# The second phase of a retention and two-layer gated kernel in a new order: early weight casts a chain ahead, x loads and block 5's eviction moved

## The chip, the cores and the metric

One core of a Trainium2 chip runs the whole program. The metric is the device time of one execution in microseconds (us). PE is the matrix engine TensorE, DVE is VectorE, ACT is ScalarE, POOL is GpSimd, and SP is SyncE, which here issues every DMA. PEld is the loading of weights into PE.

## What is computed

The program is three computations in a row, on 3072 tokens of 512 features:

```python
attn_out = _attn_ref(q, k, v)                      # decayed linear attention, 4 batches, 8 heads
x = transpose(attn_out).reshape(3072, 512)
h = x @ w_in;  x = (h * sigmoid(1.702 * h)) @ w_out          # 2048 wide
y = (sigmoid(x @ w_gate) * (x @ w_val)) @ w_out2             # 1536 wide
```

The change touches the last line, and the seam between the last two. All matrices are float32.

## The kernel before, in words

**Two phases.** The first (`units`, lines 702 to 754) works off attention and the first gated layer, six blocks of 512 tokens, and stores its result x to the DRAM tiles `x2d0` to `x2d5`. The second (lines 758 to 805) computes the last layer from them in three groups `g` of 1024 tokens, two blocks each. Every float32 product is made of three matmuls: each operand is split into a rounded high part and a low part (a cast on ACT, then a subtraction on DVE or POOL), and high times high, low times high and high times low are summed in a PSUM bank. In names, a final h or l tells the parts: `oh` and `ol` are the layer's weights, `xoh` and `xol` its input, `g2h` and `g2l` the gated values, `woh` and `wol` the output weights.

**Rounds and chains.** A group has three rounds `r`, and a round four chains: gate and value (`m` 0 and 1) for each of two pairs `p`. They are numbered through from 0 to 35; this text calls the four of a round its first to fourth chain. A chain multiplies a 2 by 2 block matrix by another with seven block products instead of eight (a Winograd scheme), each of six matmuls of 512 columns. In the order of PE: A11 B11 (`begin`), A12 B21, S2 T2, S1 T1, S3 T3 (`middle`), A22 T4, S4 B22 (`finish`). S1 to S4 are sums of weight blocks, made by `sums` on POOL; T1 to T4 are sums of x blocks. Intermediate results are taken off the bank `pa` between products: `m1` after A11 B11, `u2` after S2 T2 and `u3` after S3 T3, each a copy on ACT. The product that follows on the same bank adds to it and must wait for the copy.

**Weights of a chain.** `load_chain` brings them (`raw8`), `sums` adds the S blocks, and `split_chain` casts them in two pieces: the early one (S1, S2, A11, A12; 1024 columns; `oh0`, with the low part `ol0` by DVE) and the late one (S3, A22, S4; 768 columns; `oh1`, with `ol1` by POOL). The early piece of chain n + 1 is cast at the head of chain n's `middle`:

```python
        ahead = n + 1 < len(chains)
        if ahead and n > 0:
            rest = split_chain(n + 1, False)
```

and `rest()`, DVE's subtraction, follows before S1 T1. The results of four blocks of a chain go through `consume`: a sigmoid for a gate chain, and for a value chain a multiply by it, a cast to `g2h` and a subtraction to `g2l`. `split_out2` makes `woh` (ACT) and `wol` (POOL) from the loaded `wor`, at the end of each chain.

**The end of a round.** The last chain's `finish` stands among the output products (`out_products`): eight blocks of 128 tokens (`tt`), each over the round's four pieces of 128 features, in three rotating banks `po`. `evict` copies or adds each to `part`; in a group's last round it adds into `ost2` and stores to the output. There, `prep_x` of the next group is drawn in between: it loads x blocks (`xt`), forms T1 to T4 on POOL and splits them, in steps that `next(xs)` takes, two after each eviction.

**Order.** Every engine works off its instructions in the order in which the program lists them (`manual_schedule`), and so does SP with the DMAs. A tile that takes the place of an earlier one waits for all accesses of that one.

## Time and profile before

| | us |
|---|---|
| median of 3 runs | 1241.9 |
| lowest and highest run | 1239.98, 1242.96 |
| the profiled execution | 1237.37 |
| its span | 1235.6 |
| PE busy in the span | 1191.6 |
| DVE, ACT, POOL busy | 815.1, 537.8, 537.4 |

The span runs from the first to the last instruction; 1.8 us of the execution lie around it. Matmul records overlap: one lasts about 0.39 us, and the next begins about 0.23 us after it began, so PE counts as busy without a pause. A row of the timeline gives the start, the duration, the engine, the line, the operation with what it writes and reads, and in brackets the idle time of the engine before it and what ended that. In the list of waits a row names who waited for whom, the sum, how often, and the longest.

### The profile page before, as it was taken

To read this page: it belongs to the slowest core of one execution; us is meant where nothing else is said; L and a number is where in the kernel's file an instruction comes from. 1 tells how busy PE (TensorE), PEld (TensorE's weight loads), DVE (VectorE), ACT (ScalarE), POOL (GpSimd) and SP (SyncE) were. 2 spreads that over 40 slices of the span, in tenths; PEclk is the share of its full clock that TensorE was granted. 3 is DMA by queue.
4 is the path that set the end of the run, shared out by engine and by line. 5 is a ranking of instruction groups with operands and counts; after the bars stand their busy time and mean duration, and the time that the engine had idled before them with its cause. 6 is when DMAs were issued, how large, how long until landed. Compare 5 with 4: busy or idle time off the path is not lost.

```text
span 1235.6 us, 15997 instructions
## 1 busy us (share of the span) xinstructions
PE 1191.6 (96%) x5916; PEld 947.7 (77%) x5916; DVE 815.1 (66%) x1049; ACT 537.8 (44%) x948; POOL 537.4 (43%) x398
## 2 busy tenths in 40 slices
PE   6899999999999999999998999998999999999998
PEld 5666768877788787787886787876787877787877
DVE  5999998788687777765782626366636366535454
ACT  5334444344444444444553535253626163626151
POOL 4666773323232332322464616165616156625230
PEclk9899999999999999999999999999999999999999
DMA  8554244533334424303002202033202033212111
GB/s 301 202 175 151 84 154 161 198 117 134 118 119 137 137 94 157 125 18 103 26 1 86 85 25 75 25 107 128 77 26 78 25 97 117 91 37 63 41 35 68
DMA packets 62430, 123.47 MB, mean 100 GB/s; under 512 B 6800, under 2 KB 16016, under 8 KB 62352
## 3 DMA queue, kind: packets, MB, share of 16 engines
q1 hardware_dynamic: 62352, 122.46, 29.9%
q8 instruction: 46, 0.75, 0.2%
q14 instruction: 32, 0.26, 0.1%
HBM read 98.31 MB, written 24.12 MB: 99 GB/s over the span
## 4 chain that ended last, share of the span: by engine, by line
PE 73%; DVE 10%; issue 6%; POOL 4%; ACT 3%; DMA 3%; SPq 1%; POOLq 0%; DVEq 0%; ACTq 0%
PE pa L512 15%; PE acc L379 5%; PE pd L512 5%; PE h L275 5%; PE h L273 5%; PE h L274 5%; PE acc L380 5%; PE acc L381 5%; PE po L630 4%; PE po L629 4%; PE po L628 4%; PE pb L512 3%; DVE cva L236 2%; PE acc L375 2%; DVE g2l L542 1%
## 5 line engine op out<-in xcount | busy, mean ns | idle before, releaser
L266 POOL TENSOR_TENSOR wl<-wraw,wh 128x512 fp32r<-128x512 f32 x112 | 161.4, 1442 | 327.7 <-ACT wh L265 321.8
L273 PE MATMUL h<-xh,wh 128*128 128x512 f32 x384 | 155.4, 405 | 2.7 <-DVE xl L190 1.3
L275 PE MATMUL h<-xh,wl 128*128 128x512 f32 x384 | 152.6, 397 | 0.1
L274 PE MATMUL h<-xl,wh 128*128 128x512 f32 x384 | 151.8, 395 | 0.2 <-DVE xl L190 0.2
L380 PE MATMUL acc<-gh,wl 128*128 128x512 f32 x352 | 138.8, 394 | 4.8 <-POOL wl L266 4.8
L379 PE MATMUL acc<-gh,wh 128*128 128x512 f32 x352 | 142.4, 405 | 0.8 <-ACT sg L283 0.8
L381 PE MATMUL acc<-gl,wh 128*128 128x512 f32 x352 | 137.3, 390 | 0.0
L283 ACT ACTIVATE sg<-h 128x512 f32<-128x512 f32 x88 | 52.6, 598 | 188.7 <-PE h L275 188.5
L504 POOL TENSOR_TENSOR ol<-raw,oh 128x768 fp32r<-128x768 f32 x36 | 67.3, 1871 | 153.5 <-ACT oh L501 153.5
L512 PE MATMUL pa<-xoh,oh 128*128 128x512 f32 x288 | 115.0, 399 | 15.4 <-ACT u L571 11.0
L512 PE MATMUL pa<-xoh,ol 128*128 128x512 f32 x288 | 113.3, 393 | 0.8 <-DVE ol L504 0.8
L512 PE MATMUL pa<-xol,oh 128*128 128x512 f32 x288 | 113.8, 395 | 0.0
L628 PE MATMUL po<-woh,g2h 128*128 128x512 f32 x288 | 112.5, 391 | 1.2 <-DVE ost L521 1.2
L630 PE MATMUL po<-woh,g2l 128*128 128x512 f32 x288 | 112.5, 390 | 0.0
L629 PE MATMUL po<-wol,g2h 128*128 128x512 f32 x288 | 112.4, 390 | 0.0
L265 ACT CAST wh<-wraw 128x512 fp32r<-128x512 f32 x184 | 111.5, 614 | 0.2
L289 ACT CAST gh<-sg 128x512 fp32r<-128x512 f32 x88 | 54.6, 621 | 101.8 <-DVE sg L284 101.8
L284 DVE TENSOR_TENSOR sg<-h,sg 128x512 f32<-128x512 f32 x88 | 60.5, 687 | 54.4 <-ACT sg L283 54.4
L273 PEld LDWEIGHTS h<-xh,wh 128*128 128x128 f32 x384 | 72.8, 189 | 21.1 <-DVE xl L190 1.5
L275 PEld LDWEIGHTS h<-xh,wl 128*128 128x128 f32 x384 | 72.7, 189 | 19.0 <-POOL wl L266 1.5
L274 PEld LDWEIGHTS h<-xl,wh 128*128 128x128 f32 x384 | 72.7, 189 | 18.1 <-issue 1.9
L296 DVE TENSOR_TENSOR gl<-sg,gh 128x512 fp32r<-128x512 f32 x88 | 71.8, 816 | 17.2 <-ACT gh L289 17.2
(115 smaller groups left out, 2523.0 us busy)
## 6 DMA issues: line engine op xcount, KB each, us to landing
w<-in_w_dram SPq DMA_DIRECT2D x68, 512.0 KB, 3.6
in_t<-in_qkv_dram SPq DMA_DIRECT2D x96, 256.0 KB, 3.6
raw<-w2d SPq DMA_DIRECT2D x72, 256.0 KB, 3.1
w2d<-cva SPq DMA_DIRECT2D x36, 256.0 KB, 2.2
wor<-w2d SPq DMA_DIRECT2D x36, 256.0 KB, 2.6
xt<-x2d SPq DMA_DIRECT2D x24, 256.0 KB, 4.1
out_dram<-ost SPq DMA_DIRECT2D x24, 256.0 KB, 2.0
x2d<-ost SPq DMA_DIRECT2D x18, 256.0 KB, 2.9
```

Of the source, the lines that this page charges most:

```text
L265: nc.scalar.copy(wh, raw)
L266: lo_engine.tensor_tensor(out=wl, in0=raw, in1=wh, op=ALU.subtract)
L273: nc.tensor.matmul(bank[:, :n], wh[:, k, :], xh[:, k, :n], start=(k == 0), stop=False)
L274: nc.tensor.matmul(bank[:, :n], wh[:, k, :], xl[:, k, :n], start=False, stop=False)
L275: nc.tensor.matmul(bank[:, :n], wl[:, k, :], xh[:, k, :n], start=False, stop=(k == KC - 1))
L379: nc.tensor.matmul(a, wh[:, wc], gh[:, :n], start=st, stop=False)
L380: nc.tensor.matmul(a, wl[:, wc], gh[:, :n], start=False, stop=False)
L381: nc.tensor.matmul(a, wh[:, wc], gl[:, :n], start=False, stop=sp)
L512: nc.tensor.matmul(bank, w[:, kk], x[:, k, :], start=start and k == 0 and w is wh and x is xh, stop=stop and k == 1 and w is wl, skip_grou ...
L628: nc.tensor.matmul(bank, gh, wh, start=f == 0, stop=False)
L629: nc.tensor.matmul(bank, gh, wl, start=False, stop=False)
L630: nc.tensor.matmul(bank, gl, wh, start=False, stop=f == FR - 1)
```

## The change

It does five things in the second phase. The early cast of chain n + 2 is issued in `finish` of chain n, before the last cast or sigmoid of that chain (for the chain after a round's last, after the eviction of block 4), and only DVE's subtraction stays in `middle`. `split_out2` of a chain moves into the next chain's `middle`, behind the copy `u2`. In a round's last chain the low parts `g2l` are made in another order, the piece of the first token half first. The loads of `prep_x` are issued at the start of the third chain of a group's last round instead of the fourth, seven of them at once, three into a new pool `xu`, and its first two steps run before the last `finish`. The eviction of block 5 goes to `xt` tiles and stands behind `load_chain(1)` and `load_out(0)`. The first chain's special order (`begin` of the second chain after its `finish`) goes, and `sg`, `u2` and `c22` lose a buffer each.

```diff
@@ -380,10 +380,16 @@
             nc.tensor.matmul(a, wl[:, wc], gh[:, :n], start=False, stop=False)
             nc.tensor.matmul(a, wh[:, wc], gl[:, :n], start=False, stop=sp)
         w_t.pop((i, "out"), None)
-        if not sp:
-            return
+        if sp and i + 1 < len(units):
+            evict1(b, f)
+
+    def evict1(b, f):
+        acc = acc_t[b]
         for c in range(4):
-            t = half_t[b][c] if b in half_t else half_tile(c) if b < 2 else half_tile(3)
+            if b == len(blocks1) - 1:
+                t = p2["xt"].tile([P, 512], F32, name="xt", tag="xt")
+            else:
+                t = half_t[b][c] if b in half_t else half_tile(c if b < 2 else 3)
             if b in half_t:
                 nc.vector.tensor_tensor(out=t, in0=acc[c], in1=half_t[b][c], op=ALU.add)
             elif c % 2:
@@ -418,6 +424,7 @@
 
     def open_late():
         p2["w"].append(pool(ctx, "wo", 1, "left"))
+        p2["xu"] = pool(ctx, "xu", 3, "left")
         for name, bufs in (("g2", FR), ("wout", FR), ("part", TOK), ("tmp", 2)):
             p2[name] = pool(ctx, name, bufs, "left")
 
@@ -434,12 +441,24 @@
             [p2["x"].tile([P, 2, 512], F32R, name=f"{n}{j}", tag=f"{n}{j}") for n in ("xoh", "xol")] for j in range(7)
         ]
         xo[g] = hl
+        raws = [{}, {}]
+
+        def load(k, *js):
+            for j in js:
+                half, kk = {B11: (0, k), B12: (1, k), B22: (1, k + 2), B21: (0, k + 2)}[j]
+                name = "xu" if g and k and j != B21 else "xt"
+                raws[k][j] = p2[name].tile([P, 512], F32, name=name, tag=name)
+                nc.sync.dma_start(out=raws[k][j], in_=x2d[2 * g + half][:, kk, :])
+
+        load(0, B11, B12, B22, B21)
+        if g:
+            load(1, B11, B12, B22)
+        yield
         for k in range(2):
-            raw = {}
-            for j, half, kk in ((B11, 0, k), (B12, 1, k), (B22, 1, k + 2), (B21, 0, k + 2)):
-                raw[j] = p2["xt"].tile([P, 512], F32, name="xt", tag="xt")
-                nc.sync.dma_start(out=raw[j], in_=x2d[2 * g + half][:, kk, :])
-            yield
+            raw = raws[k]
+            if k:
+                load(1, *((B21,) if g else (B11, B12, B22, B21)))
+                yield
             for j in (T1, T2):
                 raw[j] = p2["xt"].tile([P, 512], F32, name="xt", tag="xt")
 
@@ -525,7 +544,7 @@
         g, r, p, m = chains[n]
         if m == 0:
             yield
-            sgt[p, which] = sg = tmp("sg", 5)
+            sgt[p, which] = sg = tmp("sg", 4)
             nc.scalar.activation(out=sg, in_=c, func=AF.Sigmoid)
             yield
             yield
@@ -542,7 +561,7 @@
         nc.vector.tensor_tensor(out=gl, in0=c, in1=gh, op=ALU.subtract)
         yield
 
-    carried = []
+    carried, whole, early = [], [], {}
 
     def begin(n):
         if n >= len(chains):
@@ -558,8 +577,8 @@
         a, m1 = cb[n]
         b, d = bank2("pb"), bank2("pd")
         ahead = n + 1 < len(chains)
-        if ahead and n > 0:
-            rest = split_chain(n + 1, False)
+        if ahead and (n + 1) not in early:
+            early[n + 1] = split_chain(n + 1, False)
         product(n, b, A12, B21, True, True)
         add(b, b, m1)
         while carried:
@@ -567,19 +586,20 @@
         c11 = consume(n, 0, b)
         next(c11)
         product(n, a, S2, T2, False, True)
-        u2 = tmp("u2", 2)
+        u2 = tmp("u2", 1)
         nc.scalar.copy(u2, a)
+        if whole:
+            whole.pop()
+            split_out2()
         next(c11)
-        if ahead and n > 0:
-            rest()
+        if ahead:
+            early.pop(n + 1)()
         product(n, d, S1, T1, True, True)
         product(n, a, S3, T3, False, True)
-        u3, c22 = tmp("u3", 1), tmp("c22", 2)
+        u3, c22 = tmp("u3", 1), tmp("c22", 1)
         nc.scalar.copy(u3, a)
         next(c11)
         add(c22, d, u3)
-        if n == 0:
-            split_chain(1, False)()
         cb[n] = [a, d, u2, c22]
 
     def finish(n, last):
@@ -589,12 +609,17 @@
         product(n, a, A22, T4, False, True)
         next(x22)
         next(x21)
-        next(x22)
+        if not last:
+            next(x22)
         product(n, d, S4, B22, False, True)
         next(x21)
+        if last:
+            next(x21)
         add(d, d, u2)
         next(x12)
-        next(x21)
+        next(x22 if last else x21)
+        if not last and n + 2 < len(chains):
+            early[n + 2] = split_chain(n + 2, False)
         next(x12)
         if last:
             next(x12)
@@ -757,6 +782,7 @@
 
         load_chain(1)
         load_out(0)
+        evict1(*units[-1])
         sums(1)
         xs = iter(())
         for n, (g, r, p, m) in enumerate(chains):
@@ -765,21 +791,21 @@
             load_chain(n + 2)
             if more:
                 load_out(n + 1)
-            if last and r == NR - 1 and g + 1 < NG:
+            if not last and r == NR - 1 and p == PAIRS - 1 and g + 1 < NG:
                 xs = prep_x(g + 1)
                 next(xs)
             middle(n)
             if n + 2 < len(chains) and not (last and r == NR - 1):
                 sums(n + 2)
+            if last:
+                for _ in range(2):
+                    next(xs, None)
             if not last:
-                if n > 0:
-                    begin(n + 1)
+                begin(n + 1)
                 rest = split_chain(n + 1, True)
                 finish(n, False)
                 rest()
-                split_out2()
-                if n == 0:
-                    begin(n + 1)
+                whole.append(n)
                 continue
             rest = split_chain(n + 1, True) if more else lambda: None
             split_out2()
@@ -798,10 +824,12 @@
                 evict(g, r, tt, ob[tt])
                 next(xs, None)
                 next(xs, None)
+                if tt == 5 and n + 2 < len(chains) and r == NR - 1:
+                    sums(n + 2)
+                if tt == 4 and n + 2 < len(chains) and r < NR - 1:
+                    early[n + 2] = split_chain(n + 2, False)
             for _ in xs:
                 pass
-            if n + 2 < len(chains) and r == NR - 1:
-                sums(n + 2)
             begin(n + 1)
```

**Place 1: ACT, from chain 5 (second of its round) into chain 6 (third).** `g2h` are the casts of chain 5's results, `oh0` is an early cast, `u2` chain 6's copy. Before:

```order
L540 CAST g2h_6650<-c22_6676 128x512
L540 CAST g2h_6650<-pa_6595 128x512
L540 CAST g2h_6648<-pd_6637 128x512
L617 CAST woh_6717<-wor_6551 128x512
L501 CAST oh0_6728<-raw8_6631 128x1024
L571 COPY u2_6745<-pa_6683 128x512
L529 ACTIVATE sg_6747<-pb_6726 128x512
```

and with the change:

```order
L559 CAST g2h_6649<-c22_6679 128x512
L559 CAST g2h_6649<-pa_6598 128x512
L520 CAST oh0_6718<-raw8_6633 128x1024
L559 CAST g2h_6647<-pd_6639 128x512
L590 COPY u2_6744<-pa_6686 128x512
L642 CAST woh_6746<-wor_6557 128x512
L548 ACTIVATE sg_6750<-pb_6728 128x512
L600 COPY u3_6765<-pa_6686 128x512
```

The cast of 1024 columns and `woh` no longer stand between the last `g2h` and `u2`; the cast stands one `g2h` earlier, and is one for chain 7, as the one before was, and `woh` follows `u2`.

**Place 2: SP, at the seam of the phases.** `x2d5` are the stores of block 5, `raw8` the weights of a chain, `wor` output weights. Before:

```order
L393 DMA x2d5_127<-ost_6041 128x512
L393 DMA x2d5_127<-ost_6044 128x512
L393 DMA x2d5_127<-ost_6047 128x512
L393 DMA x2d5_127<-ost_6050 128x512
L483 DMA raw8_6072<-w2d_130 128x2x256
L483 DMA raw8_6072<-w2d_130 128x512
L611 DMA wor_6075<-w2d_130 128x512
L483 DMA raw8_6080<-w2d_130 128x2x256
L483 DMA raw8_6080<-w2d_130 128x512
```

and with the change:

```order
L502 DMA raw8_6063<-w2d_130 128x2x256
L502 DMA raw8_6063<-w2d_130 128x512
L636 DMA wor_6066<-w2d_130 128x512
L399 DMA x2d5_127<-xt_6068 128x512
L399 DMA x2d5_127<-xt_6071 128x512
L399 DMA x2d5_127<-xt_6074 128x512
L399 DMA x2d5_127<-xt_6077 128x512
L502 DMA raw8_6083<-w2d_130 128x2x256
L502 DMA raw8_6083<-w2d_130 128x512
```

The loads for chain 1 and the first `wor` stand ahead of the four stores, and those of chain 2 behind.

**Place 3: DVE, in the last chain of the first group and after it.** `c22`, `pa` and `pd` are the chain's results, `xol0` to `xol6` low parts of the next group's x, `ost2` evictions. Before:

```order
L521 TENSOR_TENSOR c22_7332<-pd_7293,u3_7331 128x512
L538 TENSOR_TENSOR c22_7332<-c22_7332,sg_7247 128x512
L538 TENSOR_TENSOR pa_7229<-pa_7229,sg_7255 128x512
L542 TENSOR_TENSOR g2l_7307<-c22_7332,g2h_7306 128x512
L521 TENSOR_TENSOR pd_7293<-pd_7293,u2_7315 128x512
L538 TENSOR_TENSOR pd_7293<-pd_7293,sg_7258 128x512
L542 TENSOR_TENSOR g2l_7307<-pa_7229,g2h_7306 128x512
L542 TENSOR_TENSOR g2l_7305<-pd_7293,g2h_7304 128x512
L521 TENSOR_TENSOR ost2_7393<-po_7343,part_6446 128x512
L452 TENSOR_TENSOR xol0_7271<-xt_7284,xoh0_7270 128x512
L452 TENSOR_TENSOR xol1_7273<-xt_7290,xoh1_7272 128x512
```

and with the change:

```order
L540 TENSOR_TENSOR c22_7341<-pd_7301,u3_7340 128x512
L471 TENSOR_TENSOR xol0_7189<-xt_7202,xoh0_7188 128x512
L471 TENSOR_TENSOR xol1_7191<-xt_7208,xoh1_7190 128x512
L557 TENSOR_TENSOR c22_7341<-c22_7341,sg_7278 128x512
L557 TENSOR_TENSOR pa_7260<-pa_7260,sg_7286 128x512
L561 TENSOR_TENSOR g2l_7312<-pa_7260,g2h_7311 128x512
L540 TENSOR_TENSOR pd_7301<-pd_7301,u2_7320 128x512
L557 TENSOR_TENSOR pd_7301<-pd_7301,sg_7292 128x512
L561 TENSOR_TENSOR g2l_7312<-c22_7341,g2h_7311 128x512
L561 TENSOR_TENSOR g2l_7310<-pd_7301,g2h_7309 128x512
L540 TENSOR_TENSOR ost2_7410<-po_7360,part_6449 128x512
```

Two x subtractions come ahead of the chain's multiplies, and the low part of `pa` comes ahead of that of `c22`.

## Rows read from the trace of the kernel before

**Rows 1.** Busy time by engine (PE, PEld, DVE, ACT, POOL), second phase.

```profile
659.50:1235.60 576.10, 554.99 (x2389) 446.25 (x2387) 296.26 (x373) 241.94 (x400) 248.28 (x196) 1.00 0.21 69
```

**Rows 2.** List of waits, PE, from 655 us to the end.

```profile
PE pa L512 <- ACT u L571: 11.0, 11, 1.7
PE pa L512 <- ACT m L553: 2.3, 2, 1.2
PE pa L512 <- ACT oh L501: 1.4, 1, 1.4
PE po L628 <- DVE ost L521: 1.2, 2, 0.8
...
PE pa L512 <- DVE ol L504: 0.8, 1, 0.8
```

**Rows 3.** Timeline of PE, third chain of the second round.

```profile
751.98 0.39 PE L512 MATMUL pd<-xoh,ol 128*128 128x512 f32 x1
753.29 0.50 PE L512 MATMUL pa<-xoh,oh 128*128 128x512 f32 x1 [0.92 <-ACT u L571]
753.62 0.40 PE L512 MATMUL pa<-xol,oh 128*128 128x512 f32 x1
```

**Rows 4.** Timeline of ACT, same place.

```profile
750.70 0.59 ACT L540 CAST g2h<-pd 128x512 fp32r<-128x512 f32 x1 [2.49 <-DVE pd L538]
751.18 0.62 ACT L617 CAST woh<-wor 128x512 fp32r<-128x512 f32 x1
751.70 1.05 ACT L501 CAST oh<-raw 128x1024 fp32r<-128x1024 f32 x1
```

**Rows 5.** Timeline of DVE, same place.

```profile
747.49 1.83 DVE L542 TENSOR_TENSOR g2l<-c,g2h 128x512 fp32r<-128x512 f32 x1
...
749.96 0.70 DVE L538 TENSOR_TENSOR pd<-pd,sg 128x512 f32<-128x512 f32 x1
...
751.77 0.68 DVE L542 TENSOR_TENSOR g2l<-pd,g2h 128x512 fp32r<-128x512 f32 x1
752.78 1.47 DVE L504 TENSOR_TENSOR ol<-raw,oh 128x1024 fp32r<-128x1024 f32 x1 [0.33 <-ACT oh L501]
```

**Rows 6.** Timeline of POOL, same place.

```profile
746.92 1.85 POOL L504 TENSOR_TENSOR ol<-raw,oh 128x768 fp32r<-128x768 f32 x1 [1.20 <-ACT oh L501]
751.88 1.28 POOL L618 TENSOR_TENSOR wol<-wor,woh 128x512 fp32r<-128x512 f32 x1 [3.11 <-DMA raw<-w2d]
753.12 1.72 POOL L489 TENSOR_TENSOR raw<-raw 128x256 f32<-128x256 f32 x1
```

**Rows 7.** Timeline of POOL and DVE at two places of the first phase.

```profile
65.79 1.59 POOL L256 TENSOR_TENSOR wraw<-cva,cvb 128x512 f32<-128x512 f32 x1
65.82 0.41 DVE L233 TENSOR_SCALAR cva<-cva 128x512 uint32<-128x512 uint32 x1
...
162.13 1.30 POOL L266 TENSOR_TENSOR wl<-wraw,wh 128x512 fp32r<-128x512 f32 x1
162.15 1.55 DVE L233 TENSOR_SCALAR cva<-cva 128x512 uint32<-128x512 uint32 x1
```

**Rows 8.** First change of group: timeline of SP and DVE; DMA issues of the page.

```profile
843.56 1.81 SPq L441 DMA_DIRECT2D xt<-x2d  x4
848.73 0.68 DVE L521 TENSOR_TENSOR ost<-po,part 128x512 f32<-128x512 f32 x1
xt<-x2d SPq DMA_DIRECT2D x24, 256.0 KB, 4.1
```

**Rows 9.** Seam of the phases: timeline of POOL, SP and PE; DMA issues of the page.

```profile
655.56 2.52 POOL L266 TENSOR_TENSOR wl<-wraw,wh 128x512 fp32r<-128x512 f32 x2 [3.92 <-ACT wh L265]
666.83 1.18 SPq L483 DMA_DIRECT2D raw<-w2d  x2
669.99 0.50 PE L512 MATMUL pa<-xoh,oh 128*128 128x512 f32 x1 [0.68 <-ACT u L578]
raw<-w2d SPq DMA_DIRECT2D x72, 256.0 KB, 3.1
```

## The prediction

> **What bounds the kernel now.** I read the second phase alone, since the change leaves the first one's work as it is. The busy times of that stretch come first [rows 1]: PE works for 555.0 of 576.1 us, DVE, ACT and POOL for half of it or less. So PE sets the time, and only its pauses, some 21 us, can be won. The list of waits names them [rows 2]: 17 waits with 16.7 us of idle time, and one more of 0.7 that comes up under (c), 18 with 17.4; 14 of them are for copies that ACT takes off the bank `pa` (`u` of L571 and L578, `m`). The timeline of one of them shows what a wait costs [rows 3]: from 751.98 to 753.29 are 1.31 us and on to 753.62 another 0.33, where two matmuls would have begun 0.23 apart; that is 1.18 for 0.92 of idle time, or the idle time and 0.26. With that, all 18 cost 17.4 + 18 x 0.26 = 22.1 us, the most that this change can give.
>
> They lie at three places. (a) The third chain of each of the nine rounds waits for `u2`: the 11.0 us of [rows 2] less two waits of 1.7, so 7.6 + 9 x 0.26 = 9.9. (b) The two changes of group have those two, two for `m` (2.3) and two for `ost` (1.2): 6.9 + 6 x 0.26 = 8.5. (c) The seam of the phases has the other three, 2.9 + 3 x 0.26 = 3.7.
>
> **(a) The casts around `u2`.** ACT begins `g2h` at 750.70, then works off `woh` and the cast of 1024 columns [rows 4], and only then `u2`, which keeps PE until 753.29 [rows 3]. The new order of place 1 has neither ahead of `u2`: it starts where `woh` did, at 751.18, and takes what `g2h` takes, 0.59, until 751.77. PE could use it from 752.21 (751.98 + 0.23), so this wait goes, with 0.44 to spare. The moved cast falls into the 2.49 us in which ACT idled ahead of 750.70 [rows 4], and takes 1.05 of them. In a gate chain the cast must follow POOL's sums, and POOL now has `wol` in front of these: `wol` from at most 753.6, then two sums of at most 1.28 each, is 757.4. ACT gets to the cast at about 757.1 (18 matmuls after 752.21, a sigmoid of 0.6) and must have begun it by 759.2, so that it and the last sigmoid end before the next `u2` (36 matmuls after 752.21, 760.5). That costs nothing now, and 1 us for each us of POOL beyond 1.8. A `wor` load now waits on SP for the `wol` of its own chain's `middle`; it is used a chain later, 42 matmuls or 9.7 us, and lands in about 3. The buffer that `u2` loses is free when DVE's multiply begins at 749.96 [rows 5], since the add that reads it stands ahead. These cost nothing.
>
> **What is late next** is DVE's `ol0`, which the third matmul of the next `begin` needs at 752.21 + 8 x 0.23 = 754.05. DVE's steps from 749.96 to 751.77 are 0.60 each, so it comes to `ol0` at 752.37 instead of 752.78 [rows 5]; before, it had to wait for the cast. POOL comes to `wol` at the same time: `woh` would begin 0.48 after `u2`, at 751.66, and `wol` 0.70 later (751.18 to 751.88 in [rows 4, 6]), at 752.36. The two hold each other up: DVE's 1.83 at 747.49 lasted until 0.55 after POOL's instruction had ended at 748.77, and POOL's first sum took 1.72 because `ol0` was under way [rows 5, 6]. If DVE has it first, `ol0` ends near 753.6 (about 1.2 us, from the 1.09 that it took after `wol` ended at 753.16), and PE waits for nothing. If POOL has it, `ol0` ends at 752.36 + 1.28 + 1.09 = 754.73, 0.7 late, and PE pays 1.0. Twice the trace has them as close [rows 7]: at 65.79 POOL is 0.03 ahead, and yet DVE took its plain 0.41 and POOL 1.59; at 162.13 POOL is 0.02 ahead and DVE took 1.55. Here POOL is 0.01 ahead, nearer to a tie than either. I take DVE, and keep the other as a rival.
>
> The Trainium skill (SBUF — State Buffer, section SBUF: two separate sides) says that VectorE and GpSimd arbitrate for one shared port pair as for an exclusive lock: whoever starts first has it for the whole instruction. To the letter that gives it to POOL here. The row at 162.13 agrees, the one at 65.79 does not, at least not to 0.03 us of recorded start.
>
> So (a) gives 9.9.
>
> **(b) The change of group.** Before, the second half of the next x is loaded from 843.56 on and lands 4.1 later; a subtraction on it stands ahead of the eviction of output block 4, which ends at 849.41, 0.8 after PE wanted its bank [rows 8, 2]. The rest of that work runs into the next chain, whose `m` and `u` come late. With the change the first half's four loads and three of the second half's four leave with the third chain, and two steps run before the last `finish`; the last step falls at block 5, so ACT has its x casts behind it two blocks, 24 matmuls or 5.4 us, before `begin`, and the waits for `m` and `u` go. One load is left behind the third store, a block (2.7) earlier than 843.56: 840.9, landing at 845.0. Behind it are a cast of 0.62, two subtractions of 0.6 and the eviction's 0.68: 847.5, and 848.8 if POOL holds DVE once, against a need at 848.6. So each change of group keeps between nothing and the 1.06 it had there; between the two ends I take 0.5. In the last chain, two x subtractions now stand ahead of the multiplies on DVE (place 3). They take 1.2 to 2.5 us, but the output blocks put 12 matmuls, 2.7 us, between, and the low part that is wanted first is made first. That costs nothing. (b) gives 8.5 - 1.0 = 7.5.
>
> **(c) The seam.** Chain 1's loads leave at 666.83, behind the four stores [rows 9]. Put ahead of them they wait only for tiles that POOL has read for the last time by 658.08 [rows 9]. Landing (0.6 for the second issue, 3.1), two sums of at most 1.28, the cast of 1.05 and `ol0` of 1.2 make 666.6; PE is done with S3 T3 of the chain before, and so comes to that chain, at 669.3, where its wait of 0.68 for `u3` began [rows 9]. `begin` of chain 1 now also stands between `u3` and the product that waited for it, six matmuls or 1.4 us against 0.7. All three waits go: 3.7. At worst the load still comes late and nothing is won.
>
> The other order of the low parts removes no wait that the list shows, so nothing.
>
> **Sum:** 9.9 + 7.5 + 3.7 = 21.1. The profiled execution took 1237.4 (its span 1235.6 and 1.8 around it) and would take 1216.3. It is 4.5 below the median of the runs, and below the lowest; I take the same 21.1 off the median: **1220.8**. A measurement of this kernel can tell about 0.2%, 2.5 us, from no change.
>
> **Rivals.** *POOL gets in first* in the third chains: nine times 1.0 comes back, and 12.1 are won: 1229.8. For it speaks the 0.01 by which POOL is ahead; against it the row at 65.82. *The x work only changes its place*: with two steps in the last chain and the last load still behind a store, the waits of (b) stay, 12.6 to 13.6 are won: 1228.8. For it speaks that POOL's and DVE's x work is as much as before and that they hold each other up (1.83 and 1.72 in [rows 5, 6]); against it the loads' head start. *POOL keeps the port*: if in the third chain `wol` and then both sums pass before DVE's `ol0`, it ends at 753.64 + 2 x 1.28 + 1.09 = 757.3, and PE pays 3.25 + 0.26 nine times, 31.6: slower than before by 10.5, at 1252.4. It decides from the point where `ol0` ends more than 2.1 us late (21.1 over nine, less 0.26). Against it: at 753.12 POOL had to wait for DVE after a single instruction [rows 6]. *The change doesn't do what it says*: the early cast waits for late sums, the loads for tiles, and what is won and lost cancels, within 2.5 of 1241.9. For it speaks only that so many waits were re-made at once.
>
> **Numbers.** The forecast has 0.55, POOL first 0.22, the x work 0.10, both of these or another partial loss (1232 to 1238) 0.03, no effect 0.05, POOL keeps the port or some other new wait 0.05. Faster by over 0.2%: 0.90; within 0.2%: 0.05; slower: 0.05. The range runs from 1216.5 (all 22.1 won, and 3 us of spread as in the runs shown) to 1230.0, which takes in the first two rivals.
>
> **What would show it.** In the list of waits of the changed kernel, `u` of L590 is gone or below 1 us in total, and `oh` and `m` are gone; ACT's row order in a third chain is `g2h`, `u2`, `woh`; there DVE's `ol` (L523) takes about 1.2 and POOL's `wol` (L643) some 2.3. If POOL is first, the list has nine waits of `pa` for DVE `ol` of 0.7 instead. At the changes of group at most one wait for `ost` is left in each. I am wrong if PE waits in every chain, for the early weights or for `u2`, or if PE's matmuls follow each other more slowly than 0.23 us.

## The result, and the profile after

The changed kernel takes 1221.03 us (median of 4 runs, 1219.88 to 1221.65), the kernel before 1240.94 (4 runs, 1237.44 to 1242.96): a ratio of 0.9842, with a 95% interval from 0.9825 to 0.9859. The forecast was 1220.8. The profiled execution took 1219.88, its span 1218.1; against 1237.37 of the one before that is 17.5 us less, where the sum of the prediction had 21.1. So the forecast met the time more closely than its terms deserve. That closeness is luck, and the terms are what the rest looks at.

PE's list of waits from 655 us to the end in the changed kernel (who waited for whom: total us, times, longest):

```profile
PE po L653 <- DVE ost L540: 3.1, 6, 1.0
PE acc L380 <- POOL wl L266: 0.8, 1, 0.8
```

The second row belongs to the first phase and is as before. Of [rows 2], `u`, `m`, `oh` and `ol` are gone altogether; the wait for `ost` has grown from twice to six times and from 1.2 to 3.1 us. Busy time by engine in the second phase, to be read beside [rows 1] (stretch, length, then PE, PEld, DVE, ACT, POOL with counts, granted clock, DMA share, GB/s):

```profile
659.60:1218.10 558.50, 551.70 (x2389) 447.48 (x2387) 294.53 (x373) 241.34 (x400) 251.98 (x195) 1.00 0.22 70
```

The work is the same, the clock too; PE pauses for 6.8 us instead of 21.1. How fast the first phase was differs by up to 2.7 us between profiled executions of kernels that don't change it, so from here on I compare executions by the **second phase's length**: from the start of the matmul that ends PE's last wait for `wl` to the end of the span. That matmul on the timeline of PE, in the kernel before and in the changed one:

```profile
656.88 0.50 PE L380 MATMUL acc<-gh,wl 128*128 128x512 f32 x1 [0.84 <-POOL wl L266]
```

```profile
656.97 0.50 PE L380 MATMUL acc<-gh,wl 128*128 128x512 f32 x1 [0.85 <-POOL wl L266]
```

So the length was 1235.6 - 656.88 = 578.7 and is 1218.1 - 656.97 = 561.1: 17.6 us less. The lists account for it: 18 waits of 17.4 us with 0.26 each, 22.1, against six of 3.1, 4.7; the difference is 17.4.

**The third chain.** ACT there, in the second round (start, duration, engine, line, operation; in brackets the idle time before and what ended it):

```profile
746.65 0.59 ACT L559 CAST g2h<-pd 128x512 fp32r<-128x512 f32 x1 [1.61 <-DVE pd L557]
747.13 0.59 ACT L590 COPY u<-pa 128x512 f32<-128x512 f32 x1
747.61 0.63 ACT L642 CAST woh<-wor 128x512 fp32r<-128x512 f32 x1
```

PE at the product that waited until 753.29 in [rows 3]:

```profile
747.86 0.39 PE L531 MATMUL pd<-xoh,ol 128*128 128x512 f32 x1
748.09 0.39 PE L531 MATMUL pa<-xoh,oh 128*128 128x512 f32 x1
```

`u2` ends at 747.72, PE takes it up at 748.09 without a pause. DVE's `ol0` and POOL's `wol` begin in the same hundredth, and DVE is not held up (the first row is of DVE's timeline, the second of POOL's):

```profile
748.32 1.22 DVE L523 TENSOR_TENSOR ol<-raw,oh 128x1024 fp32r<-128x1024 f32 x1
748.32 2.36 POOL L643 TENSOR_TENSOR wol<-wor,woh 128x512 fp32r<-128x512 f32 x1 [3.60 <-ACT woh L642]
```

It is the same in all nine rounds: 1.22 and 2.36 to 2.37, starts 0.00 apart. That is the forecast's case, and not its first rival.

**The seam.** POOL's first sums for chain 1, ACT's cast of its early weights, and DVE's low part:

```profile
658.12 0.74 POOL L508 TENSOR_TENSOR raw<-raw 128x256 f32<-128x256 f32 x1
...
664.79 1.05 ACT L520 CAST oh<-raw 128x1024 fp32r<-128x1024 f32 x1
...
666.05 1.22 DVE L523 TENSOR_TENSOR ol<-raw,oh 128x1024 fp32r<-128x1024 f32 x1
```

The loads were issued at 651.77, 15 us before those of [rows 9], and nothing waits at the seam. They left 6 us earlier than the prediction had them, and yet `ol` ends at 667.27 and not at its 666.6: ACT's cast stands behind the copies of block 5, the last of which begins at 664.31. PE comes to the first matmul that needs this `ol` at 669.74, so there is time to spare.

**The change of group** has the six waits that are left, three at each: idle times of 0.23, 0.39 and 1.03 at the first, 0.20, 0.39 and 0.84 at the second. The longest on PE, and what DVE and SP did ahead of it:

```profile
838.11 0.37 SPq L451 DMA_DIRECT2D xt<-x2d  x1
...
842.52 1.29 DVE L471 TENSOR_TENSOR xol<-xt,xoh 128x512 fp32r<-128x512 f32 x2 [3.19 <-ACT xoh L470]
843.73 0.68 DVE L540 TENSOR_TENSOR ost<-po,part 128x512 f32<-128x512 f32 x1
...
844.47 0.50 PE L653 MATMUL po<-woh,g2h 128*128 128x512 f32 x1 [1.03 <-DVE ost L540]
```

The one load that still stands behind the third store leaves at 838.11, and the eviction of block 4 stands on DVE behind the two subtractions that need it.

### The profile page after: what moved, and what is told of

The parts are those of the page before. It is cut to its first block, busy times and chain, and to the rows that moved or that the text cites. A ratio compares the mean times of both kernels' runs of the same rounds, so it can differ in the third digit from the quotient of the medians.

```text
span 1218.1 us, 16030 instructions
## 1 busy us (share of the span) xinstructions
PE 1191.2 (98%) x5916; PEld 951.6 (78%) x5916; DVE 812.6 (67%) x1049; ACT 537.1 (44%) x948; POOL 542.3 (45%) x398
## 4 chain that ended last, share of the span: by engine, by line
PE 78%; DVE 9%; issue 5%; POOL 3%; DMA 3%; ACT 2%; SPq 0%; POOLq 0%; DVEq 0%; ACTq 0%
PE pa L531 16%; PE pd L531 8%; PE acc L379 6%; PE h L275 5%; PE h L273 5%; PE h L274 5%; PE acc L380 5%; PE acc L381 5%; PE po L653 4%; PE po L655 4%; PE po L654 4%; PE pb L531 4%; DVE cva L236 3%; PE h L144 1%; PE h L185 1%
## 5 line engine op out<-in xcount | busy, mean ns | idle before, releaser
L643 POOL TENSOR_TENSOR wol<-wor,woh 128x512 fp32r<-128x512 f32 x36 | 56.9, 1582 | 88.9 <-ACT woh L642 88.9
```

## The experiments

All twelve start from the changed kernel. "Length" is that of the second phase, 561.1 in the changed kernel; a median stands beside the interval of its ratio to the kernel before, which ran beside each group of four.

| kernel | median, us | ratio to before, 95% | span | length | against 561.1 |
|---|---|---|---|---|---|
| e1 late cast | 1227.64 | 0.9893 to 0.9921 | 1227.3 | 567.7 | +6.6 |
| e2 woh back | 1223.14 | 0.9858 to 0.9886 | 1221.7 | 562.8 | +1.7 |
| e12 both | 1229.75 | 0.9905 to 0.9930 | 1227.2 | 570.3 | +9.1 |
| e3 memset of 64 | 1221.19 | 0.9843 to 0.9872 | 1218.6 | 561.0 | -0.1 |
| e5 memset of 320 | 1221.63 | 0.9832 to 0.9863 | 1219.1 | 561.6 | +0.5 |
| e10 copy from PSUM | 1229.36 | 0.9900 to 0.9927 | 1228.4 | 569.6 | +8.4 |
| e6 x undone | 1222.04 | 0.9836 to 0.9864 | 1219.8 | 562.6 | +1.4 |
| e9 x and sums undone | 1225.03 | 0.9863 to 0.9893 | 1223.1 | 565.3 | +4.2 |
| e7 seam loads undone | 1229.70 | 0.9897 to 0.9925 | 1228.5 | 570.5 | +9.4 |
| e11 token order undone | 1225.15 | 0.9864 to 0.9891 | 1224.0 | 564.5 | +3.4 |
| e4 B21 load ahead | 1217.59 | 0.9814 to 0.9841 | 1215.6 | 558.6 | -2.5 |
| e8 and x steps spread | 1215.85 | 0.9785 to 0.9813 | 1214.0 | 555.9 | -5.2 |

### What held u2 up: e1, e2, e12

e1 takes the early cast back to the head of `middle`:

```diff
-        if not last and n + 2 < len(chains):
-            early[n + 2] = split_chain(n + 2, False)
...
-                if tt == 4 and n + 2 < len(chains) and r < NR - 1:
-                    early[n + 2] = split_chain(n + 2, False)
```

> The changed kernel with the 1024-column cast of the early weights taken back to the head of the chain that prepares them, so that it stands on ACT between g2h and u2 in a third chain; woh stays behind u2. Theory (the cast and woh each held up u2, one after the other): u2 begins one cast, about 1.0 us, later than in the changed kernel, against 1.5 in the kernel before, so PE waits 0.92 less woh's 0.52, or 0.40 us, in each third chain, 0.66 us of time with the restart, some 5.3 to 5.9 us over the rounds: about 1226 to 1227 us. Rival (moving woh alone did it): no wait for u2, within 1 us of the changed kernel's 1221.

ACT in the third chain of the second round of e1:

```profile
750.01 0.59 ACT L559 CAST g2h<-pd 128x512 fp32r<-128x512 f32 x1 [2.57 <-DVE pd L557]
750.49 1.05 ACT L520 CAST oh<-raw 128x1024 fp32r<-128x1024 f32 x1
751.44 0.59 ACT L590 COPY u<-pa 128x512 f32<-128x512 f32 x1
```

The list has `PE pa` waiting for `u` nine times again, 4.3 us in total, 0.48 each: +6.6. The theory had 0.40 and 5.3 to 5.9.

e2 takes `woh` and `wol` back to the end of the chain before:

```diff
-        if whole:
-            whole.pop()
-            split_out2()
...
-                whole.append(n)
+                split_out2()
```

> The changed kernel with the cast woh and its subtraction wol taken back to the end of the chain before, so that woh stands on ACT between g2h and u2; the early cast stays where the change has it. Theory: u2 begins 0.5 us later and still ends about 0.1 us before PE wants it, so no wait for u2, or at most 0.1 us; but wol now comes to POOL while DVE is in the two subtractions ahead of ol. If DVE keeps the port through them, nothing is lost: within 1 us of 1221. If POOL gets in between, ol ends about 0.8 us late and nine times 1.06 us come back: about 1230. Rival (woh alone was what held up u2): waits for u2 of 0.9 us in nine chains, about 1231.

On PE's timeline the matmul behind `u2` begins 0.44 after the one before it in the first round and 0.36 or 0.37 in the other eight, instead of 0.23: too little to be listed. POOL's `wol` now starts 0.48 ahead of `ol` and gets through first (timeline of DVE and POOL):

```profile
750.04 0.68 DVE L561 TENSOR_TENSOR g2l<-pd,g2h 128x512 fp32r<-128x512 f32 x1
750.15 1.29 POOL L640 TENSOR_TENSOR wol<-wor,woh 128x512 fp32r<-128x512 f32 x1 [3.11 <-ACT woh L639]
750.63 1.89 DVE L523 TENSOR_TENSOR ol<-raw,oh 128x1024 fp32r<-128x1024 f32 x1
```

POOL did get in between, as the expectation feared, but began so early that `ol` ended at 752.52 and PE's matmul on it began in its turn, at 752.60; only the next one is 0.09 late. So e2 costs 1.7, not 9. That is a net figure: e2 has only four waits for `ost`, 2.3 us in total. Those of block 0 at the two changes of group are gone, and with their 0.26 that is worth 1.3.

e12 undoes both.

> The changed kernel with both moves around u2 undone, the cast of 1024 columns and woh with wol; all else stays. Theory: PE waits for u2 again in each third chain, 0.92 us and 0.26 for the restart, together 9.9 us: about 1231. Rival (the two undone alone gave 6.4 and 2.0; if they only add up): 1229.5.

PE waits for `u` nine times, 8.3 us in total, 0.92 or 0.93 each, as in [rows 2, 3]: +9.1. By these waits it would be 10.6 (8.3 + 9 x 0.26), but block 0's two waits for `ost` are gone here too, worth 1.4. Alone they gave 6.6 and 1.7. `u2` was 0.92 late behind two casts that hold ACT for about 0.5 and 0.95 us; with the longer one gone 0.05 to 0.14 is left of that (e2), with the shorter one gone 0.48 (e1).

### Who gets the shared port: e3, e5, e10

These set one more instruction on DVE in front of `ol` in each third chain, so that `wol` begins first:

```diff
+        if n % 4 == 2:
+            nc.vector.memset(p2["tmp"].tile([P, 64], F32, name="gap", tag="gap", bufs=1), 0.0)
         if ahead:
             early.pop(n + 1)()
```

e3 has it as it stands, e5 with 320 columns, e10 with `tensor_copy(gap, b[:, :192])`, which reads the bank `pb`.

> The changed kernel with one more DVE instruction, a memset of 64 columns of about 0.1 us, ahead of DVE's ol in each third chain, so that POOL's wol begins about 0.1 us before ol instead of in the same moment. Theory (the one that begins first keeps the shared port): wol takes its plain 1.3 us, ol ends about 1.1 us after it, 0.7 us later than PE wants it, and PE waits nine times, 0.95 us each with the restart: 8 to 9 us more, about 1230. Rival (DVE gets the port whoever begins first): wol takes 2.3 us, ol 1.2, and the time is that of the changed kernel, 1221.

`wol` begins 0.07 before `ol` and takes 2.38, `ol` 1.16; the length stays. With 0.07 us the question was still open.

> As the kernel with the memset of 64 columns, but with 320 columns, about 0.33 us, so that POOL's wol begins some 0.3 us before DVE's ol in each third chain. With 64 columns wol began 0.07 us ahead by the records and still took 2.38 us, ol 1.16, and the time did not move. Theory (whoever gets to the port first keeps it, and POOL gets there later than its recorded start by more than 0.07 us): at 0.3 us POOL has it, wol takes 1.3, ol ends 1.1 after it, some 0.5 us after PE wants it, and nine waits of 0.5 with 0.26 each for the restart cost 6.9 us: about 1228. Rival (DVE has precedence whoever begins first): wol takes over 2.3 us, ol 1.2 and ends 0.3 us before PE wants it: 1221.

POOL and DVE at the same place of e5:

```profile
748.92 2.63 POOL L645 TENSOR_TENSOR wol<-wor,woh 128x512 fp32r<-128x512 f32 x1 [3.60 <-ACT woh L644]
749.02 0.33 DVE L596 MEMSET gap<- 128x320 f32 x1
749.26 1.16 DVE L523 TENSOR_TENSOR ol<-raw,oh 128x1024 fp32r<-128x1024 f32 x1
```

`wol` begins 0.10 ahead of the memset and 0.34 ahead of `ol`, and ends 1.13 after `ol`: it had no part of the port while DVE was at the two. By this alone DVE would seem to have precedence, the rival's case.

> As the kernels with a memset ahead of DVE's ol in each third chain, but with a copy of 192 columns from a PSUM bank in its place, some 0.3 us, so that DVE has nothing to do with two SBUF operands or an SBUF fill while POOL's wol begins. Theory (POOL begins first and keeps the shared port; the memset of the other kernels held it for DVE): wol takes about 1.3, ol is held until some 1.1 us after it, 0.4 to 0.5 us too late for PE: nine times 0.7 us, about 1227. Rival (DVE has precedence also here): wol over 2.3, ol 1.2: 1221.

The same place in e10, with the matmul of PE that waits:

```profile
751.13 1.29 POOL L645 TENSOR_TENSOR wol<-wor,woh 128x512 fp32r<-128x512 f32 x1 [3.60 <-ACT woh L644]
751.58 0.36 DVE L596 COPY gap<-pb 128x192 f32<-128x192 f32 x1 [0.37 <-ACT sg L548]
751.86 1.65 DVE L523 TENSOR_TENSOR ol<-raw,oh 128x1024 fp32r<-128x1024 f32 x1
...
753.56 0.50 PE L531 MATMUL pa<-xoh,ol 128*128 128x512 f32 x1 [0.67 <-DVE ol L523]
```

The copy waited for ACT's sigmoid, which I had not reckoned with, so POOL is 0.73 ahead of `ol` instead of 0.3. It keeps the port for its plain 1.29, `ol` ends 1.09 after it, and PE waits nine times, 6.2 us in all: +8.4. That is the first rival of the prediction on the chip, 1229.36 us where it had 1229.8. DVE has no precedence: a DVE instruction with two SBUF operands that is already under way keeps POOL out, and POOL under way keeps DVE out. What sets e3 and e5 apart is the memset, as the theory of e10 has it, and not a head start that was too short. The kernel before has `wol` 0.34 ahead of `ol` as well, with a multiply on a bank in front of `ol` instead of a memset, and there POOL has the port (first row POOL, second DVE):

```profile
679.60 1.29 POOL L618 TENSOR_TENSOR wol<-wor,woh 128x512 fp32r<-128x512 f32 x1
679.94 2.03 DVE L504 TENSOR_TENSOR ol<-raw,oh 128x1024 fp32r<-128x1024 f32 x1
```

The fourteen traces have 81 places where POOL begins an operation of 512 columns 0.01 to 0.49 us ahead of a DVE instruction with two SBUF operands, and the DVE instruction before that one reads a bank. In all 81 POOL took its plain 1.27 to 1.30. In the 68 where the two begin together, or DVE up to 0.05 ahead, POOL was held up. With a memset in front POOL was held up 18 times of 18, 0.07 and 0.34 ahead. Why a memset that itself begins 0.10 behind POOL keeps it out is not shown.

### The change of group: e6, e9, e4, e8

e6 loads and works x as before (four loads in the last chain, four behind the fourth store, no step ahead of `finish`; its expectation speaks of the third store, but SP has four stores ahead of these loads, in e6 as in the kernel before):

```diff
-            if not last and r == NR - 1 and p == PAIRS - 1 and g + 1 < NG:
+            if last and r == NR - 1 and g + 1 < NG:
...
-            if last:
-                for _ in range(2):
-                    next(xs, None)
...
-        if g:
-            load(1, B11, B12, B22)
```

> The changed kernel with the next group's x loaded and worked as before: the first four loads in the last chain, the second four behind the third output store, all in the same six buffers, no step ahead of the last finish; the early casts, woh behind u2 and the seam stay. Theory: the waits for m, u and ost at the two changes of group come back, 8.5 us in place of the 4.9 that the changed kernel still has there, so 3.6 more: about 1224.8. Rival (the x work only changes its place): within 1 us of 1221.

Its waits: `m` twice, 2.3 in total, and `ost` twice, 2.9 in total. The two for `u`, 1.7 each in [rows 2], did not return, and it costs 1.4, not 3.6. In e6 POOL comes to the sums of the next chain before its own last x subtraction, since the sums stand at block 5:

```profile
848.67 1.18 POOL L505 TENSOR_TENSOR raw<-raw 128x256 f32<-128x256 f32 x1
849.93 1.62 POOL L506 TENSOR_TENSOR raw<-raw 128x512 f32<-128x512 f32 x1
...
852.66 1.29 POOL L468 TENSOR_TENSOR xol<-xt,xoh 128x512 fp32r<-128x512 f32 x1
```

e9 puts the sums back behind all of x:

```diff
-                if tt == 5 and n + 2 < len(chains) and r == NR - 1:
-                    sums(n + 2)
...
             for _ in xs:
                 pass
+            if n + 2 < len(chains) and r == NR - 1:
+                sums(n + 2)
```

> As the kernel with the x loads and steps undone (1222.0, where the two waits of 1.7 us for u had not come back), with the sums of the chain after next also put back behind all the x work, instead of at block 5. Theory, formed after that run: the waits for u came from the sums, which stood on POOL behind its last x subtraction, and with them the 1024-column cast ahead of u2; they come back, twice 1.7 and 0.26: about 1225.9. Rival (the waits for u went with the early casts): no wait for u, 1222.

ACT and PE at the first change of group in e9:

```profile
854.02 1.04 ACT L517 CAST oh<-raw 128x1024 fp32r<-128x1024 f32 x1 [3.19 <-POOL raw L506]
854.97 0.58 ACT L587 COPY u<-pa 128x512 f32<-128x512 f32 x1
...
855.61 0.50 PE L528 MATMUL pa<-xoh,oh 128*128 128x512 f32 x1 [1.70 <-ACT u L587]
```

Both waits for `u` are back (3.4 in total), 2.8 us more than e6. So those waits came from the sums: late on POOL, they kept ACT in the cast that stands ahead of `u2`. Early sums alone remove them (e6). That early x would do it with the sums behind it is not shown, since no run has that. The changed kernel has both: its diff also moves the sums from behind the x work to block 5, which the list of its five things leaves out.

e4 issues the load that was left behind the third store, `B21` of the second half, a step earlier, into the same tile:

```diff
             split(B21, nc.vector)
+            if g and not k:
+                load(1, B21)
...
-                load(1, *((B21,) if g else (B11, B12, B22, B21)))
+                if not g:
+                    load(1, B11, B12, B22, B21)
```

> The changed kernel with the one load of the next group's x that still stood behind the third output store issued a step earlier, in the last chain, into the same buffer. Theory (that load makes the subtractions in front of the eviction of block 4 late): the waits of 1.03 and 0.84 us for ost go, 2.4 us with two restarts, about 1218.6, and the four short ones of 0.2 to 0.4 us stay. Rival (DVE has too much to do in that stretch and is late whenever the load lands): the waits move to another block and less than 1 us is won.

The load leaves at 823.13 instead of 838.11. The two long waits are gone, the four short ones left (`ost` 1.2, 4 times): -2.5, the theory's 2.4.

e8 adds this to e4:

```diff
             if last:
-                for _ in range(2):
-                    next(xs, None)
+                next(xs, None)
...
                 next(xs, None)
-                next(xs, None)
+                if tt != 1:
+                    next(xs, None)
```

> The kernel with the B21 load a step earlier (1217.6), and one step of x work fewer in the last chain and after block 1's eviction, one more after those of blocks 2 and 5, so that the evictions of blocks 0 and 2 come up sooner on DVE. Theory (the four waits left, of 0.2 to 0.4 us, are evictions that stand behind subtractions of x on DVE): all four go, 1.2 us of idle time and 4 times 0.26, so about 1215.4, and no wait for m or u comes in their place, since x was done 1.7 us before PE wanted it. Rival (the DVE work is as much, and the waits only move): within 0.7 us of 1217.6.

PE's list from 655 us in e8:

```profile
PE acc L380 <- POOL wl L266: 0.8, 1, 0.8
```

Not one wait of PE is left in the second phase, and the length is 5.2 below the changed kernel's. At 1215.85 us it is the fastest kernel here. It moves two steps at once, and which of them removed which wait was not tried singly.

### The seam and the token order: e7, e11

e7 puts block 5's eviction back in front of chain 1's loads:

```diff
-        if sp and i + 1 < len(units):
+        if sp:
             evict1(b, f)
...
-        evict1(*units[-1])
```

> The changed kernel with block 5's eviction back in front of chain 1's loads (and in its former buffer); all else stays, also that chain 1 is now begun before chain 0 is finished. Theory: the loads leave after the four stores, at about 667, and their oh comes at about 674.4 as before, but PE now wants it some 4 us earlier than before, since begin(1) stands ahead of the last products of chain 0: one wait of 4 us or a little more and one of up to 1 for ol, 4 to 6 us: 1225 to 1227. Rival (the loads would land in time behind the stores too): 1221.

SP, ACT and PE in e7:

```profile
663.65 4.21 SPq L396 DMA_DIRECT2D x2d<-ost  x4
667.95 1.20 SPq L499 DMA_DIRECT2D raw<-w2d  x2
...
674.78 1.04 ACT L517 CAST oh<-raw 128x1024 fp32r<-128x1024 f32 x1 [7.26 <-POOL raw L506]
675.73 0.58 ACT L587 COPY u<-pa 128x512 f32<-128x512 f32 x1
...
676.36 0.80 PE L528 MATMUL pa<-xoh,oh 128*128 128x512 f32 x1 [7.28 <-ACT u L587]
```

The loads and the cast come when I expected them, but PE waits earlier than I expected: chain 1's cast now stands ahead of chain 0's own `u2` on ACT, and PE is held at S3 T3, a product before it comes to chain 1. One wait of 7.28, +9.4. The wait and its 0.26 make 7.5 of that. The rest is PE's clock. After this pause of 7.28 us the granted clock is 0.50, the lower level of 1.2 GHz, and it is 1.00 again from 680.80 on (stretch, length, engines as in [rows 1], granted clock, DMA share, GB/s):

```profile
676.40:680.00 3.60, 3.60 (x9) 2.86 (x10) 0.99 (x2) 1.00 (x2) 2.80 (x2) 0.50 0.00 0
```

From 676.36 to 680.73 PE begins ten matmuls, most of them 0.43 apart; after a short wait they take 0.33 + 9 x 0.23 = 2.4. So these 4.37 us hold 2.0 that the wait itself does not show.

e11 gives the low parts of a round's last `finish` their old order:

```diff
-        if not last:
-            next(x22)
+        next(x22)
         product(n, d, S4, B22, False, True)
         next(x21)
-        if last:
-            next(x21)
         add(d, d, u2)
         next(x12)
-        next(x22 if last else x21)
+        next(x21)
```

> The changed kernel with the low parts in a round's last finish in their former order (c22's third step ahead of the product S4, and not behind it). Theory (the order removes no wait): within 0.7 us of 1221, no new wait. Rival (the first output blocks need the other half's low part sooner): a wait of po for g2l in each round, 0.3 us or more with the restart, over 2.5 us in all: 1224 or more.

The rival's case: seven of nine rounds wait for `g2l`, 6.0 us in total, and the length grows by 3.4, since the six waits for `ost` fall away in turn. POOL, DVE and PE at the end of the second round of e11:

```profile
766.53 0.70 DVE L557 TENSOR_TENSOR pa<-pa,sg 128x512 f32<-128x512 f32 x1 [1.67 <-PE pa L531]
766.68 1.85 POOL L523 TENSOR_TENSOR ol<-raw,oh 128x768 fp32r<-128x768 f32 x1
767.14 1.94 DVE L561 TENSOR_TENSOR g2l<-c,g2h 128x512 fp32r<-128x512 f32 x1
...
771.07 0.50 PE L652 MATMUL po<-woh,g2l 128*128 128x512 f32 x1 [0.63 <-DVE g2l L561]
```

The subtraction from `c`, which has both operands in SBUF, falls behind POOL's `ol`, is held for 1.2 us, and everything on DVE behind it is late. In the changed kernel the one from the bank `pa` stands there, and both take their plain times (POOL, then DVE):

```profile
763.77 1.84 POOL L523 TENSOR_TENSOR ol<-raw,oh 128x768 fp32r<-128x768 f32 x1
...
764.95 0.69 DVE L561 TENSOR_TENSOR g2l<-pa,g2h 128x512 fp32r<-128x512 f32 x1 [0.65 <-ACT g2h L559]
```

In the kernel before, POOL was further on when DVE came there (timeline of POOL and DVE):

```profile
768.24 1.85 POOL L504 TENSOR_TENSOR ol<-raw,oh 128x768 fp32r<-128x768 f32 x1
768.90 0.70 DVE L538 TENSOR_TENSOR pa<-pa,sg 128x512 f32<-128x512 f32 x1 [1.77 <-PE pa L512]
769.51 1.12 DVE L542 TENSOR_TENSOR g2l<-c,g2h 128x512 fp32r<-128x512 f32 x1
```

`ol` began 0.66 ahead of that multiply, in e11 0.15 behind it: the `wol` that was moved into the chain now stands on POOL ahead of the sums. With that `wol` put back (e2 and e12) POOL's `ol` is again 0.63 and 0.69 ahead of the multiply. So before, the subtraction was held for 0.4 us only, and PE did not wait.

## Why the prediction was right, and where its terms were not

**(a), 9.9 us: right.** All nine waits for `u2` are gone, and e12 gives 9.1 back. Of the "0.44 to spare" 0.37 were there (748.09 less 747.72). The moved cast, the sums behind `wol` and the `wor` loads cost nothing in the chains, as reckoned: no wait for any of them is listed. But the moved `wol` has a part in what went wrong under (b): with it put back (e2, e12), block 0's waits for `ost`, 0.23 and 0.20, are gone.

**Who is first at the port: right, by luck.** I took DVE because the near-tie at 65.82 went to it; DVE had the port nine times of nine. But the row at 65.82 is of another instruction, with one input, and where POOL is 0.03 ahead of that one it had the port 21 times of 32 in the fourteen traces. What the choice hung on was a hundredth of a us: the prediction had POOL 0.01 ahead, and at 0.01 ahead a place in e6 went to POOL; measured was 0.00, and at 0.00 it was DVE each time. So 0.22 was too little for the rival. The price of the other outcome is now measured, 8.4 us, where the rival had 9.0. The Trainium skill (SBUF — State Buffer, section SBUF: two separate sides) gives the lock to whoever starts first, among GpSimd instructions and such VectorE instructions as use a two-port mode or have two SBUF inputs. e2 and e11 agree on the kind of instruction: beside POOL the subtraction from a bank took its plain 0.68, the one from `c` 1.94. On "first" the 81 and 68 places above agree with it, to 0.01 us of recorded start. The memset of e3 and e5 kept POOL out from behind; whether it is one of the rule's two-port instructions is not shown.

**(b), 7.5 us: the mechanism was half right, the size wrong.** It gave 3.8: 8.5 were there, and 3.1 and 6 times 0.26 are left, 4.7, where I had left 1.0. These 3.7 are, to 0.2, the 3.5 by which the sum of 21.1 was above the 17.6 measured. My sign for it, "at most one wait for `ost`" at each change, failed too: there are three. Two steps failed.
- That "two x subtractions now stand ahead of the multiplies on DVE", at no cost. They took 2.25 us, within the 1.2 to 2.5 that I gave them, but POOL also held up the multiply and the low part of `c` behind them, which take 0.7 plain:

```profile
821.44 2.25 DVE L471 TENSOR_TENSOR xol<-xt,xoh 128x512 fp32r<-128x512 f32 x2
823.60 1.77 DVE L557 TENSOR_TENSOR c<-c,sg 128x512 f32<-128x512 f32 x1
...
828.58 1.57 DVE L561 TENSOR_TENSOR g2l<-c,g2h 128x512 fp32r<-128x512 f32 x1
```

That is 2.25 + 1.07 + 0.87 = 4.2 us, against the 2.7 that I had put between. DVE evicted block 0 at 830.67, without a pause behind the chain's last low part, and block 2 at 836.97, behind two subtractions that took 2.88 beside POOL. These are the four waits of 0.2 to 0.4; in e8 one step fewer in the chain and one fewer behind block 1 remove them.

- "840.9, landing at 845.0", so that a change of group keeps 0.5. The load stands behind the third store (before, behind the fourth), and that store was itself late, since block 2's eviction was. It left 2.4 later in its place than I had it (PE wants that bank at 843.44, 5.2 sooner than the 848.68 before, and 838.11 + 5.2 = 843.3), almost as late as before, 843.56. The wait stayed at 1.03 and 0.84. e4 shows that the load alone was its cause.

I also put the waits for `u` down to late x. They came from the sums behind x on POOL (e9 against e6, 2.8 us); the loads ahead, the part that the change is named after, are worth 1.4 there (e6), and 6.7 with the load and the steps as e8 has them (562.6 less 555.9).

**(c), 3.7 us: right.** But e7 says more than the prediction did: the loads ahead are not only a gain of 3.7. Without them the new order of chain 1 costs 9.4 (e7), 2.0 of it at PE's lower clock; that is more than the seam cost before. I had weighed the new order of the seam only with the loads in time.

**"The other order of the low parts removes no wait that the list shows, so nothing."** True of the list before, and wrong of the change. It removes a wait that the rest of the change makes: `wol` moved into the chain, so POOL's `ol` is later there and meets the low part of `c`. It covers 3.4 us (e11), and the prediction should have named it as that cover.

**Time and sum.** The profiles differ by 17.5, the medians by 19.9. I had taken 21.1 off the median of three runs, 1241.9; a fourth run of 1237.44 brought it to 1240.94. The closeness of 1220.8 to 1221.03 is a sum that was 3.6 too high and a starting point that lay 4.5 above the profile it was worked out from, where the changed kernel's median lies 1.2 above its own; the two errors cancel, by luck. (By its own terms the lower end of the range would be 1216.8, not 1216.5.)

**The other rivals.** *The x work only changes its place* was near the truth for the waits of `ost`, but not for `m` and `u`. *POOL keeps the port* through the sums as well did not occur: even in e10 and e2, where POOL was first, DVE came next after one instruction. *The change doesn't do what it says* did not occur either: 17.6 us were won.

## What to carry to other kernels

Casts and a copy in a row on one engine can often be moved so that what the bottleneck waits for goes first; look then at what the moved work now meets on the port that two engines share. Two parts here, the token order, costed at nothing, and the seam's loads, costed at 3.7, also held a wait shut that another part of the change opened. Undo each part singly from the finished change: the sum of what the four give back (9.1, 4.2, 9.4 and 3.4) is well over the 17.6 that all of it gave, and the surplus is the cover that they give each other, and in e7 PE's lower clock. And where an eviction frees the bottleneck's bank, count every instruction in front of it on its engine at its held-up duration, not at its plain one: with one load and two steps moved so that the evictions come up in time, another 5.2 us were won (e8).

## What the runs showed of the hardware

- Between a POOL operation and a DVE instruction with two SBUF operands, the recorded starts decide to 0.01 us who has the port: POOL ahead by 0.01 to 0.49, it took 1.27 to 1.30 (81 places); together or DVE ahead, POOL was held up (68 places, 2.36 for `wol` in the changed kernel).
- A DVE memset between the two is the exception. In e5 it begins 0.10 behind `wol`, and `wol`, 0.34 ahead of `ol`, ends 1.13 after it. DVE's instructions overlap by 0.06 to 0.09 us in the records (`ol` at 749.26 begins before the memset's end at 749.35), and POOL did not get in between them.
- After a pause of PE of 7.28 us (e7) the granted clock was 0.50 and matmuls began 0.43 us apart instead of 0.23.
- DVE subtractions with one operand in a PSUM bank run beside POOL at full speed (0.68 and 1.29 in e2); with both in SBUF they are held until POOL's instruction ends (1.89 in e2, 1.94 in e11).
- The first phase, which no kernel here changes, ended between 656.9 and 659.6 us in the profiled executions. With differences of 1 to 3 us to tell apart, the second phase's own length was the steadier measure; by it e6 and e2, 1 and 2 us apart from the changed kernel in the medians, are 1.4 and 1.7.
